# One x tile loaded behind wq instead of two ahead of it, the K folds in one row, the first keys right behind them

## The chip, the cores and the metric

The kernel runs on one core of a Trainium2 chip. The metric is the device time of one launch in microseconds (us), lower is better; a quoted time is the median of several runs. The profile's span, from the first to the last recorded instruction, is about 1.25 us shorter than the time of the same run (297.35 against 296.1).

Every profiled run has a granted clock of 1.0.

## The reference, cut to what matters

```python
qkv = x @ wqkv                                  # x: 2048 x 640, wqkv: 640 x 1920
pq, pk = einsum(q, w_phi), einsum(k, w_phi)     # per head, 32 heads of 20
phi_q = concat(softmax(pq), softmax(-pq)); phi_k likewise
kv = einsum(phi_k, v);  z = sum(phi_k)          # linear attention state
a = ((phi_q @ kv) / (phi_q @ z + 1e-6)) @ wo
b = (gelu(x @ w_gate) * (x @ w_up)) @ w_down
g = sigmoid((x * gate_w).sum(-1))
return g * a + (1 - g) * b
```

Since `q` and `k` are used only through `w_phi`, the kernel multiplies ("folds") `w_phi` into the q and k parts of `wqkv`. For this it needs both parts transposed, `wkT` and `wqT`. All of x is needed transposed as well (`xT`, 16 tiles of 128 rows). Tiles 0 to 3 are transposed by TensorE; tiles 4 to 15, `wkT` and `wqT` come through transposing DMAs, all issued by the SP queue.

## The kernel before: what the change touches

```python
def loads(self):                      # the order on the SP queue
    xload("sp", 0)                    # x tiles 0, 1, plain (2, 3: ACT queue)
    ...                               # five plain loads of the v weights
    xturn(4, 2)                       # transposing load of x tiles 4, 5
    wload(self.wkT, D, "wkT")         # transposing load, 640 x 640
    xturn(6, 2)                       # x tiles 6, 7
    wload(self.wqT, 0, "wqT")
    xturn(8, 4)
    xturn(12, 4)
    ...                               # weights of the feed-forward part

def fold(self, kt, which, banks, ekey):
    # six small matmuls of wT (k or q) with the block diagonal of w_phi, then one
    # copy out of PSUM into w3 (k) or wq2 (q), by VectorE ("d") or ScalarE ("a")
    ...

def attention_state(self):
    warm(7)                           # seven matmuls of zeros ahead of the work
    ...                               # transposes of x tiles 0..3, V of tiles 0..3
    self.v_early(4, 6)                # V projection of tile 4 into banks 6, 7
    self.v_early(5, 0)
    f(0, "k", (2, 3), "d")
    f(1, "k", (4, 5), "a")
    self.v_early(6, 6)
    f(2, "k", (2, 3), "d")
    f(3, "k", (4, 5), "a")
    f(4, "k", (0, 1), "d")
    self.v_early(7, 6)
    self.k_early(0, 2)                # K projection of tile 0, then two exponents on ScalarE
    f(0, "q", (4, 5), "d")
    f(1, "q", (6, 7), "d")
    ...                               # two folds, k_early(1), two folds, k_early(2), ...
    self.k_norm(0)                    # VectorE normalises phi_k of tile 0: 3.58 us
    self.k_early(3, 0)
    self.k_norm(1)
    self.pq(0, 1, 1)                  # Q product, banks 6/7 in turn, two exponents each
    self.pq(0, 0, 0)
    self.pq(0, 3, 3)
    self.gram(0)                      # phi_k^T v of tile 0, accumulated over all tiles
    self.k_norm(2)
    self.pq(0, 2, 2)
    ...
    for t in range(4, NT):            # projections of tile t, k_norm(t), Q products, and
        ...                           # Gram up to tile t-3 (t < 8), later up to tile t-2
```

A bank (0 to 7) is a part of PSUM, the memory that TensorE's products land in; copying a bank out is called evacuating it, and a product that needs the bank waits for that. A helper records every operation with the buffers that it reads and writes and places the waits. The names of the trace's lines are therefore those of helpers: L280 transposes of x, L350 V of tiles 0 to 3, L341 projection, L321 fold, L303 the gate column, L434 Gram, L486 Q product, L217 and L213 the transposing loads of x and of wk/wq. After the change everything behind the new method moves down by 9 lines (Gram is L443, the Q product L495), and L371 is that method.

The softmax here doesn't subtract the row's maximum and nothing guards it: scores larger than these inputs give would overflow.

## Time and profile before

| | before |
|---|---|
| time, 3 runs | 296.21 us (295.81 to 296.45) |
| the profiled run itself | 297.35 us, span 296.1 |
| PE busy | 291.0 us (98%) |
| V of tile 4 starts | 11.30 us |
| wait for x tiles 6 and 7 | 1.39 us |

The page's share of busy time shows that TensorE (PE) is the busiest by far (PEld is its weight load, DVE VectorE, ACT ScalarE, POOL GpSimd):

```profile
span 296.1 us, 4789 instructions
PE 291.0 (98%) x1904; PEld 169.1 (57%) x1904; DVE 162.7 (55%) x321; ACT 104.2 (35%) x183; POOL 27.8 (9%) x56
```

The timeline of PE in the block that the change touches (columns: start, duration, engine, line, operation, output and inputs, shape, count, and in brackets the idle time before it and what ended it):

```profile
4.47 1.29 PE L280 MATMUL ps<-ident,xtok 128*128 128x128 bf16 x20 [0.24 <-DMA xtok<-in_A_x_dram]
...
10.16 0.22 PE L303 MATMUL ps<-ident,gz 128*128 128x128 bf16 x1
...
11.30 2.88 PE L341 MATMUL ps<-w,xT 128*128 128x512 bf16 x20
14.02 0.79 PE L321 MATMUL ps<-BD,wkT 128*128 128x140 bf16 x12
16.20 1.53 PE L341 MATMUL ps<-w,xT 128*128 128x512 bf16 x10 [1.39 <-DMA xT<-in_A_x_dram]
17.57 1.11 PE L321 MATMUL ps<-BD,wkT 128*128 128x140 bf16 x18
...
29.64 1.25 PE L486 MATMUL ps<-xT,wq 128*128 128x512 bf16 x5 [0.34 <-ACT Eq L492]
```

V of tile 6 (16.20) waits 1.39 us for its transposed x. The SP queue's timeline shows why it came late: the load was issued at 10.66, behind 4.57 us of issue for wk (durations here are issue times, not data movement):

```profile
3.62 2.38 SPq L217 DMA_TRANSPOSE xT<-in_A_x_dram  x1
6.05 4.57 SPq L213 DMA_TRANSPOSE wkT<-in_A_wqkv_dram  x1
10.66 1.41 SPq L217 DMA_TRANSPOSE xT<-in_A_x_dram  x1
12.12 4.61 SPq L213 DMA_TRANSPOSE wqT<-in_A_wqkv_dram  x1
```

### The profile page before, as it was taken

To read this page: it belongs to the slowest core of one execution; us is meant where nothing else is said; L and a number is where in the kernel's file an instruction comes from. 1 tells how busy PE (TensorE), PEld (TensorE's weight loads), DVE (VectorE), ACT (ScalarE), POOL (GpSimd) and SP (SyncE) were. 2 spreads that over 40 slices of the span, in tenths; PEclk is the share of its full clock that TensorE was granted. 3 is DMA by queue.
4 is the path that set the end of the run, shared out by engine and by line. 5 is a ranking of instruction groups with operands and counts; after the bars stand their busy time and mean duration, and the time that the engine had idled before them with its cause. 6 is when DMAs were issued, how large, how long until landed. Compare 5 with 4: busy or idle time off the path is not lost.

```text
span 296.1 us, 4789 instructions
## 1 busy us (share of the span) xinstructions
PE 291.0 (98%) x1904; PEld 169.1 (57%) x1904; DVE 162.7 (55%) x321; ACT 104.2 (35%) x183; POOL 27.8 (9%) x56
## 2 busy tenths in 40 slices
PE   7989999999999999999999999999999999999997
PEld 3656565555554455766555567655556765555674
DVE  3238999998886579600777710077771007777100
ACT  3347787766773221112222211222221122222112
POOL 7000000000000011110111100012110001222000
PEclk9999999999999999999999999999999999999999
DMA  8999993000001302211011130101311000111111
GB/s 231 181 200 273 364 356 113 0 0 2 0 2 31 57 4 37 51 47 44 3 23 22 24 44 22 46 0 23 24 22 43 25 26 21 22 22 24 22 46 44
DMA packets 38224, 18.85 MB, mean 64 GB/s; under 512 B 30266, under 2 KB 37946, under 8 KB 38202
## 3 DMA queue, kind: packets, MB, share of 16 engines
q1 hardware_dynamic: 37392, 18.19, 25.0%
q10 hardware_dynamic: 810, 0.35, 0.4%
q8 instruction: 15, 0.25, 0.4%
q14 instruction: 7, 0.06, 0.1%
HBM read 9.04 MB, written 2.62 MB: 39 GB/s over the span
## 4 chain that ended last, share of the span: by engine, by line
PE 93%; SPq 3%; DMA 2%; ACT 1%; issue 0%; ACTq 0%
PE ps L594 38%; PE ps L693 19%; PE ps L341 12%; PE ps L699 8%; PE ps L486 7%; PE ps L630 4%; PE ps L434 3%; DMA xT<-in_A_x_dram 2%; SPq L213 2%; PE ps L604 1%; PE ps L672 1%; PE ps L321 1%; SPq L217 1%; SPq L226 1%; ACT Ek L400 0%; ACT Eq L492 0%
## 5 line engine op out<-in xcount | busy, mean ns | idle before, releaser
L599 DVE TENSOR_TENSOR hT<-ps,gl 128x512 bf16<-128x512 f32 x52 | 35.7, 688 | 79.8 <-PE ps L594 79.7
L594 PE MATMUL ps<-xT,wg_sb 128*128 128x512 bf16 x260 | 64.6, 379 | 0.0
L594 PE MATMUL ps<-xT,wu_sb 128*128 128x512 bf16 x260 | 64.6, 379 | 0.0
L597 ACT ACTIVATE gl<-ps 128x512 bf16<-128x512 f32 x52 | 31.1, 597 | 82.5 <-PE ps L594 80.3
L693 PE MATMUL ps<-wd_sb,hT 128*128 128x320 bf16 (+2 forms) x416 | 59.3, 299 | 0.0
L693 PEld LDWEIGHTS ps<-wd_sb,hT 128*128 128x128 bf16 x416 | 40.2, 98 | 16.8
L659 POOL TENSOR_TENSOR Og<-O,O 128x640 bf16<-128x640 bf16 x16 | 22.3, 1396 | 244.4 <-DVE O L657 244.4
L594 PEld LDWEIGHTS ps<-xT,wu_sb 128*128 128x128 bf16 x260 | 25.4, 98 | 30.7
L341 PE MATMUL ps<-w,xT 128*128 128x512 bf16 (+3 forms) x240 | 41.0, 321 | 1.4 <-DMA xT<-in_A_x_dram 1.4
L594 PEld LDWEIGHTS ps<-xT,wg_sb 128*128 128x128 bf16 x260 | 24.9, 98 | 26.4
L709 ACT ACTIVATE outsb<-ps,Gm 128x640 bf16<-128x640 f32 (+2 forms) x17 | 13.0, 763 | 71.5 <-PE ps L699 71.5
L341 PEld LDWEIGHTS ps<-w,xT 128*128 128x128 bf16 x240 | 22.3, 97 | 19.7 <-DMA xT<-in_A_x_dram 1.6
L411 DVE TENSOR_REDUCE Dk<-Ek 128x64 f32<-128x1280 bf16 x16 | 23.7, 1480 | 3.2 <-ACT gcol L403 3.2
L420 DVE TENSOR_TENSOR Ek<-Ek,Dk 128x640 bf16<-128x640 bf16 x32 | 25.0, 821 | 0.6
L486 PE MATMUL ps<-xT,wq 128*128 128x512 bf16 x100 | 24.7, 379 | 0.3 <-ACT Eq L492 0.3
L657 DVE TENSOR_TENSOR O<-ps,RH 128x640 bf16<-128x640 f32 x32 | 24.8, 815 | 0.0
L699 PE MATMUL ps<-wo_sb,goT 128*128 128x320 bf16 (+2 forms) x160 | 24.6, 299 | 0.0
L492 ACT ACTIVATE Eq<-ps 128x512 bf16<-128x512 f32 x40 | 21.7, 604 | 4.0 <-PE ps L486 4.0
L400 ACT ACTIVATE Ek<-ps 128x640 bf16<-128x640 f32 x32 | 20.7, 702 | 3.5 <-PE ps L341 3.5
L699 PEld LDWEIGHTS ps<-wo_sb,goT 128*128 128x128 bf16 x160 | 15.1, 98 | 7.2 <-issue 1.3
L630 PEld LDWEIGHTS ps<-KV,Eq 128*128 128x128 bf16 x192 | 12.0, 98 | 3.6
L630 PE MATMUL ps<-KV,Eq 128*128 128x154 bf16 x192 | 13.7, 221 | 0.0
(63 smaller groups left out, 148.4 us busy)
## 6 DMA issues: line engine op xcount, KB each, us to landing
out_dram<-outsb SPq DMA_DIRECT2D x15, 160.0 KB, 1.8
wd_sb<-in_B_w_down_dram SPq DMA_DIRECT2D x1, 2080.0 KB, 13.7
wg_sb<-in_B_w_gate_dram SPq DMA_DIRECT2D x1, 1120.0 KB, 6.1
wu_sb<-in_B_w_up_dram SPq DMA_DIRECT2D x1, 1120.0 KB, 8.5
wg_sb<-in_B_w_gate_dram SPq DMA_DIRECT2D x1, 960.0 KB, 9.8
wu_sb<-in_B_w_up_dram SPq DMA_DIRECT2D x1, 960.0 KB, 10.2
w<-in_A_wqkv_dram SPq DMA_DIRECT2D x5, 160.0 KB, 4.2
wo_sb<-in_A_wo_dram SPq DMA_DIRECT2D x1, 800.0 KB, 9.2
```

The source lines that it names most:

```text
L341: sc.op("pe", lambda e, kt=kt: e.matmul(self.bank(bank)[:, bcol:bcol + n], self.xT[:, kt, t * P:(t + 1) * P], self.w3[:, kt, c0:c0 + n], s ...
L411: sc.op("dve", lambda e: e.tensor_reduce(self.Dk[:, se, 0, :].rearrange("p (s h) -> p s h", h=H), self.Ek[:, se, :, :].rearrange("p s (h d ...
L420: sc.op("dve", lambda e, v=v, r=r: e.tensor_tensor(v, v, r, ALU.mult), reads=[("Rk", se)], writes=[("Ek", se, s)])
L486: sc.op("pe", lambda e, kt=kt: e.matmul(self.bank(bank), self.wq2[:, kt, i * P:(i + 1) * P], self.xT[:, kt, b * self.BT:(b + 1) * self.BT] ...
L594: sc.op("pe", lambda e, kt=kt, w=w, bk=bk: e.matmul(self.bank(bk), w[:, kt, c * P:(c + 1) * P], xs(kt), start=(kt == 0), stop=(kt == self. ...
L597: sc.op("act", lambda e: e.activation(self.gl[:, slot, :], self.bank(banks[0]), AF.Gelu_apprx_tanh), reads=[("ps", banks[0])], writes=[("g ...
L599: sc.op("dve", lambda e: e.tensor_tensor(self.hT[:, c, :], self.bank(banks[1]), self.gl[:, slot, :], ALU.mult), reads=[("ps", banks[1]), ( ...
L630: sc.op("pe", lambda e, s=s, i=i, n=n, o0=o0, k0=k0, bk=bk, r=r: e.matmul(self.bank(bk)[:, o0:o0 + n], self.Eq[:, s, i, t * P:(t + 1) * P] ...
L657: dve(lambda e, o=o, f=f, s=s: e.tensor_tensor(o, V[s][:, :, :, 0:DH], f, ALU.mult), rb + [key(6 + s)], [("O", s, sl)], guard=old)
L659: sc.op("pool", lambda e: e.tensor_tensor(self.Og[:, sl, :], self.O1[:, sl, :], self.O2[:, sl, :], ALU.add), reads=[("O", 0, sl), ("O", 1, ...
L693: sc.op("pe", lambda e: e.matmul(self.bank(bk, w), self.hT[:, c, tt * P:(tt + 1) * P], self.wd_sb[:, c, w0:w0 + w], start=(c == 0 and not ...
L699: sc.op("pe", lambda e: e.matmul(self.bank(bk, w), self.goT[:, gs, k, :], self.wo_sb[:, k, w0:w0 + w], start=False, stop=(k == self.KD - 1 ...
```

## The change

The intent is to take that wait away. Tile 6 is loaded with tiles 4 and 5 ahead of wk, so that three V projections can run before wk is needed; tile 7 moves behind wq and its V projection to the end of the block. All five K folds then run in a row. The first K projection follows them directly with the contraction tile as its outer loop, so that it can use each fold's copy as it comes. The Q folds are spread between the other K projections.

```diff
-        xturn(4, 2)
+        xturn(4, 3)
         wload(self.wkT, D, "wkT")
-        xturn(6, 2)
         wload(self.wqT, 0, "wqT")
+        xturn(7, 1)
         xturn(8, 4)
@@ new method
+    def k_behind(self, t, b0):
+        for kt in range(self.KD):
+            for c0, n, bk, col in ((640, 384, b0, 128), (1024, 257, b0 + 1, 0)):
+                ...                  # one matmul; waits only for ("wk2", kt)
+        self.k_evac(t, b0)
@@ attention_state
         self.v_early(4, 6)
         self.v_early(5, 0)
-        f(0, "k", (2, 3), "d")
-        f(1, "k", (4, 5), "a")
-        self.v_early(6, 6)
-        ...                          # three K folds
-        self.v_early(7, 6)
-        self.k_early(0, 2)
+        self.v_early(6, 2)
+        f(0, "k", (4, 5), "d")
+        f(1, "k", (6, 7), "a")
+        f(2, "k", (0, 1), "d")
+        f(3, "k", (2, 3), "a")
+        f(4, "k", (4, 5), "d")
+        self.k_behind(0, 6)
+        self.k_early(1, 0)
         f(0, "q", (4, 5), "d")
-        ...
+        ...                          # two q folds, k_early(2), two q folds, k_early(3), one q fold
         self.k_norm(0)
-        self.k_early(3, 0)
+        self.v_early(7, 0)
         self.k_norm(1)
         self.pq(0, 1, 1)
         self.pq(0, 0, 0)
         self.pq(0, 3, 3)
+        self.pq(0, 2, 2)
         self.gram(0)
         self.k_norm(2)
-        self.pq(0, 2, 2)
```

More of the change, by code (lines that the diff above doesn't have):

```diff
@@ L366, in v_first_evac @@
             self.sc.op("act", lambda e: e.activation(dst, src, AF.Copy), reads=rd, writes=wr)
+    def k_behind(self, t, b0):
+        for kt in range(self.KD):
+            for c0, n, bk, col in ((640, 384, b0, 128), (1024, 257, b0 + 1, 0)):
+                self.sc.op("pe", lambda e: e.matmul(
+                    self.bank(bk)[:, col:col + n], self.xT[:, kt, t * P:(t + 1) * P], self.w3[:, kt, c0:c0 + n],
+                    start=(kt == 0), stop=(kt == self.KD - 1)),
+                    reads=[("xT", t), ("wk2", kt), "wgate"], writes=[("ps", bk)], signal=(kt == self.KD - 1))
+        self.k_evac(t, b0)
     def k_early(self, t, b0):
@@ L540, in attention_state @@
         self.v_early(5, 0)
-        f(0, "k", (2, 3), "d")
-        f(1, "k", (4, 5), "a")
-        self.v_early(6, 6)
-        f(2, "k", (2, 3), "d")
-        f(3, "k", (4, 5), "a")
-        f(4, "k", (0, 1), "d")
-        self.v_early(7, 6)
-        self.k_early(0, 2)
-        f(0, "q", (4, 5), "d")
-        f(1, "q", (6, 7), "d")
-        self.k_early(1, 0)
-        f(2, "q", (4, 5), "d")
-        f(3, "q", (6, 7), "d")
-        self.k_early(2, 2)
-        f(4, "q", (4, 5), "d")
+        self.v_early(6, 2)
[6 more added lines that the diff above has]
+        self.k_early(1, 0)
+        f(0, "q", (4, 5), "d")
+        f(1, "q", (2, 3), "d")
+        self.k_early(2, 6)
+        f(2, "q", (0, 1), "d")
+        f(3, "q", (4, 5), "d")
+        self.k_early(3, 2)
+        f(4, "q", (6, 7), "d")
         self.k_norm(0)
-        self.k_early(3, 0)
+        self.v_early(7, 0)
         self.k_norm(1)
```

## The prediction

> **What bounds it now.** TensorE: the busy table gives PE 291.0 of 296.1 us, and in the chain of waits from 16.2 us to the end nearly every piece is PE. The granted clock is 1.0 throughout. So only PE idle time is to be had; in the part that the change touches (11.3 to 32.5 us) PE's timeline shows two gaps. (a) PE is idle 1.39 us before the V projection that starts at 16.20, released by the transposed load of x tiles 6 and 7: issued at 10.66, behind wk's 4.57 us of issue, it landed 5.49 us later. wk had landed at 13.35. (b) 0.34 us before the third Q product at 29.64, released by ScalarE's exponent.
>
> **What changes.** No arithmetic, bytes or number of loads. Tile 6 comes ahead of wk, tile 7 behind wq; folds and projections are reordered.
>
> *Loads.* On SP's timeline two tiles took 1.4 to 2.4 us to issue, four 3.3 to 3.5, wk and wq 4.6 each: about 0.75 us a tile. The Trainium skill (Perfetto Trace Analysis, "DMA Instruction — HWDGE") says that the reported duration ends when the descriptors are generated, not when data has moved; this trace agrees: wk's issue lasts 4.57 us, its landing takes 7.3. Landing came 2.7 to 3 us after the end of issue. My estimates: tiles 4 to 6 landed near 10.5; wk near 14.1 to 14.8 (before 13.35); wq near 18.8 (before 19.7); tile 7 near 21; tiles 8 to 15 about 1 us later, with over 15 us of slack.
>
> *TensorE.* A projection costs 1.36 us, a fold 0.315 (0.94 for three), a Q product 1.08, Gram 0.55. From 11.30: three V projections to 15.4, wk there in time by some 0.6 to 1.3 us; five K folds to about 17.0, the fifth waiting 0.1 to 0.2 for VectorE to evacuate banks 4 and 5 (0.82 a copy); the first K projection, contraction-tile-outer so that it can follow the folds' copies, waits for the last copy at about 18.3 and ends near 18.6, 0.3 late. The other K projections and the Q folds find banks, wq (needed at 20.0) and copies ready, ending near 24.3; V of tile 7 near 25.6, instead of 26.98. The Q products' exponent wait stays, 0.3 to 0.4; moving Gram 0 behind the fourth Q product adds at most 0.1. Block end near 31.0 instead of 32.5.
>
> VectorE's normalisations run back to back, 3.58 us a tile; they start about 1.3 us earlier and Gram 1 still finds its tile with 0.8 us to spare. From there on PE is unbroken, so the saving should arrive in full: 1.39 + about 0.4 of small gaps, less about 0.4 of new evacuation waits.
>
> **Predicted time: 294.8 us**, 8 in 10 between 294.1 and 296.0. Chance of faster by over 2%: 0.01; within 2%: 0.98; slower by over 2%: 0.01.
>
> **What would show it.** The wait for the transposed x tile on PE gone; V of tile 6 following tile 5 without gap; folds from 15.4; a wait of 0.1 to 0.5 us at the last K fold or inside the first K projection, released by VectorE or ScalarE; no wait on wk or wq; first Gram near 30.5; everything later shifted by the same 1.4 us; DMA and busy totals unchanged.
>
> **What would make it wrong.** wk or wq landing over 1 us later than estimated, so that the wait just moves to the folds: then 0 to 0.8 us of gain. Evacuation waits in the folds above 1 us. VectorE's normalisations, nearly saturated until 50 us, holding Gram.

## The result

| | before | after |
|---|---|---|
| time, 6 runs each | 296.33 us (295.81 to 297.44) | 296.86 us (295.92 to 297.01) |
| the profiled run, and its span | 297.35, 296.1 us | 296.78, 295.5 us |
| gate column (L303) starts | 10.16 us | 10.98 us |
| gate column to the end | 285.94 us | 284.52 us |

The ratio is 1.0005, 95% interval 0.9981 to 1.0029: the same. (A ratio here is the mean time of one kernel's fast runs over that of the other's of the same rounds, so it is not quite the ratio of the medians.) The predicted 294.8 with 294.1 to 296.0 missed; the time did not go down at all.

Yet the profile after shows nearly everything that was foretold. PE's timeline of the changed kernel:

```profile
4.56 2.06 PE L280 MATMUL ps<-ident,xtok 128*128 128x128 bf16 x20
...
10.98 0.22 PE L303 MATMUL ps<-ident,gz 128*128 128x128 bf16 x1
...
12.33 4.02 PE L341 MATMUL ps<-w,xT 128*128 128x512 bf16 x29
16.19 1.95 PE L321 MATMUL ps<-BD,wkT 128*128 128x140 bf16 x30
17.98 1.60 PE L371 MATMUL ps<-w,xT 128*128 128x384 bf16 x10
...
26.44 4.75 PE L495 MATMUL ps<-xT,wq 128*128 128x512 bf16 x20
31.03 0.71 PE L443 MATMUL ps<-Ek,vaug 128*128 128x240 bf16 x6
```

The three V projections run without a gap (x29 and not x30: one record is missing, and the true start is about 12.12), the folds follow, no DMA is waited for. The SP queue, same columns as before:

```profile
3.62 3.29 SPq L217 DMA_TRANSPOSE xT<-in_A_x_dram  x1
6.95 3.84 SPq L213 DMA_TRANSPOSE wkT<-in_A_wqkv_dram  x1
10.83 3.87 SPq L213 DMA_TRANSPOSE wqT<-in_A_wqkv_dram  x1
14.74 8.90 SPq L217 DMA_TRANSPOSE xT<-in_A_x_dram  x3
```

And the page's first lines:

```profile
span 295.5 us, 4764 instructions
PE 290.8 (98%) x1879; PEld 169.7 (57%) x1904; DVE 162.6 (55%) x321; ACT 104.5 (35%) x183; POOL 27.7 (9%) x56
```

To compare runs, cut each at a point that both kernels share and that lies ahead of the change: the start of the gate column. What comes before it is the "head", identical in both kernels; what comes after it is the "tail". Between these two profiles the tail fell by 1.42 us (285.94 to 284.52), which is the predicted 1.4. The head grew by 0.82, although the change does not touch it. So two questions are left: why does the head move, and why do the timed runs show nothing of the tail's 1.42?

### The profile page after: what moved, and what is told of

Read it like the earlier page. It is cut to its first block, busy times and chain, and to the rows that moved or that the text cites. A ratio compares the mean times of both kernels' runs of the same rounds, so it can differ in the third digit from the quotient of the medians.

```text
span 295.5 us, 4764 instructions
## 1 busy us (share of the span) xinstructions
PE 290.8 (98%) x1879; PEld 169.7 (57%) x1904; DVE 162.6 (55%) x321; ACT 104.5 (35%) x183; POOL 27.7 (9%) x56
## 2 busy tenths in 40 slices
DMA packets 38224, 18.85 MB, mean 64 GB/s; under 512 B 30266, under 2 KB 37946, under 8 KB 38202
## 4 chain that ended last, share of the span: by engine, by line
PE 97%; DMA 1%; issue 1%; ACT 0%
PE ps L603 38%; PE ps L702 19%; PE ps L341 12%; PE ps L708 8%; PE ps L495 7%; PE ps L639 4%; PE ps L443 3%; PE ps L350 2%; PE ps L613 1%; DMA xtok<-in_A_x_dram 1%; PE ps L321 1%; PE ps L681 1%; PE ps L280 1%; PE ps L371 0%; ACT Eq L501 0%
## 5 line engine op out<-in xcount | busy, mean ns | idle before, releaser
L603 PE MATMUL ps<-xT,wg_sb 128*128 128x512 bf16 x251 | 63.0, 380 | 0.5
L341 PE MATMUL ps<-w,xT 128*128 128x512 bf16 (+3 forms) x228 | 39.0, 322 | 0.1
L341 PEld LDWEIGHTS ps<-w,xT 128*128 128x128 bf16 x230 | 21.5, 97 | 17.6
L495 PE MATMUL ps<-xT,wq 128*128 128x512 bf16 x94 | 23.4, 380 | 0.4
```

The source lines that it names most:

```text
L341: sc.op("pe", lambda e, kt=kt: e.matmul(self.bank(bank)[:, bcol:bcol + n], self.xT[:, kt, t * P:(t + 1) * P], self.w3[:, kt, c0:c0 + n], s ...
L495: sc.op("pe", lambda e, kt=kt: e.matmul(self.bank(bank), self.wq2[:, kt, i * P:(i + 1) * P], self.xT[:, kt, b * self.BT:(b + 1) * self.BT] ...
L603: sc.op("pe", lambda e, kt=kt, w=w, bk=bk: e.matmul(self.bank(bk), w[:, kt, c * P:(c + 1) * P], xs(kt), start=(kt == 0), stop=(kt == self. ...
```

## The experiments

Theory A: the 1.39 us wait was an accident of the one profiled run of before; the timed runs mostly don't have it, so there is nothing to save. Theory B: the wait is typical and the gain real, but hidden by a random stretch of slow TensorE clock in the head. Theory C: the gain is real at 32 us and given back later, because VectorE's back-to-back normalisations hold the Gram products. Twelve runs were made, all correct.

All tails and heads, from PE's timeline and the span of each profile:

| run | head | tail | PE's waits for DMA behind the head |
|---|---|---|---|
| before, first profile | 10.16 | 285.94 | x tiles 6, 7: 1.39 |
| null_before | 10.34 | 284.36 | none |
| look_b2 | 10.79 | 284.41 | none |
| look_b3 | 10.66 | 284.34 | none |
| late_before | 18.61 | 284.39 | none |
| after, first profile | 10.98 | 284.52 | none |
| after_again | 10.90 | 284.60 | none |
| after_third | 10.10 | 284.60 | none |
| late_after | 18.85 | 284.55 | none |
| order_only | 10.55 | 284.55 | none |
| tuned | 11.16 | 284.34 | none |
| loads_only | 10.90 | 286.0 | x tile 7: 1.50 |
| delay_before | 10.20 | 286.8 | wk 1.02, x tiles 6, 7: 0.99 |
| delay_after | 10.21 | 285.39 | wk: 0.66 |

### 1. The kernel before again (null_before)

Edit: none; timed in 5 rounds.

> The kernel before, unchanged, timed against itself: it shows the scatter that any verdict has to be read against, and gives a second profile. Theory A (the profiled run of before had an unusually late wait for x tiles 6 and 7, 1.39 us): in this second profile that wait is shorter, under 0.8 us. Theory B (the wait is typical and the saving of about 1.4 us is real, but lost in the timed runs to an early stretch of slow TensorE clock that falls at random): the wait is again 1.2 to 1.5 us, and the timed runs fall in two groups 0.7 to 1.0 us apart. Ratio to before 1.000 within 0.003 either way.

Measured: ratio 0.9998 (0.9983 to 1.0013), 295.64 to 296.86. PE's timeline of this profile:

```profile
11.48 2.88 PE L341 MATMUL ps<-w,xT 128*128 128x512 bf16 x20
14.20 0.79 PE L321 MATMUL ps<-BD,wkT 128*128 128x140 bf16 x12
14.83 1.52 PE L341 MATMUL ps<-w,xT 128*128 128x512 bf16 x10
16.19 1.11 PE L321 MATMUL ps<-BD,wkT 128*128 128x140 bf16 x18
...
28.25 1.25 PE L486 MATMUL ps<-xT,wq 128*128 128x512 bf16 x5 [0.34 <-ACT Eq L492]
```

V of tile 6 follows the folds with no wait at all. The SP queue of the same run says why: wk took 3.80 us to issue instead of 4.57, and the load behind it was issued 0.9 us earlier and landed after 4.7 us instead of 5.49, at 14.46: 0.37 us before it was needed.

```profile
3.62 2.25 SPq L217 DMA_TRANSPOSE xT<-in_A_x_dram  x1
5.91 3.80 SPq L213 DMA_TRANSPOSE wkT<-in_A_wqkv_dram  x1
9.76 1.41 SPq L217 DMA_TRANSPOSE xT<-in_A_x_dram  x1
11.21 5.52 SPq L213 DMA_TRANSPOSE wqT<-in_A_wqkv_dram  x1
```

What follows: theory A. The same instructions have a tail of 284.36 us, 1.58 shorter than in the first profile, and 0.16 shorter than the changed kernel's.

### 2. The changed kernel again (after_again)

Edit: none; 5 rounds.

> The changed kernel, unchanged, a second time. Theory B: its runs again fall in groups 0.7 to 1.0 us apart, according to whether the 20 transposes of x by TensorE took 1.3 us (fast clock) or about 2.1 us (slow clock); over ten runs of each kernel the mean gain shows, ratio 0.996 to 0.998. Theory A: no groups needed, ratio 0.999 to 1.001, and this profile shows the same block length as the first one.

Measured: ratio 1.0004 (0.9991 to 1.0018), five runs: 296.71, 296.86, 296.63 and 296.06, 296.13. Theory B's mean gain did not come; its two groups did, and its slow transposes: the 20 took 2.22 us in this profile, which belongs to the run of 296.71.

### 3 and 4. Both kernels behind a long warm-up (late_before, late_after)

```diff
+        sc.op("dve", lambda e: e.memset(self.zero[:, :], 0.0), writes=["zero"])
+        for i in range(26):
+            sc.op("pe", ...matmul of zeros..., reads=["zero"], writes=[("ps", 0), "pre"])
         xload("sp", 0)               # now with reads=["pre"]
...
-        warm(7)
+        warm(14)
```

> The kernel before with 26 extra warming matmuls ahead of the first load, which waits for them, and 14 instead of 7 behind it: the real work starts with TensorE's clock already up, so the random stretch of slow clock is gone. Costs about 7 us, the same in both late kernels. Transposes 1.3 us in every run, timed runs within 0.5 us of each other if the clock was the scatter (theory B). Its profile shows the wait for x tiles 6 and 7: 1.2 to 1.5 us by theory B, under 0.8 by theory A.

> The changed kernel with the same late, warm start. Theory B: 1.2 to 1.6 us faster than late_before (ratio of the two 0.995 to 0.996). Theory A: within 0.5 us of late_before. Theory C (the gain is real at 32 us but VectorE's back-to-back normalisations hold the Gram products and give it back by 60 us): the block to the first Gram is 1.6 us shorter, the end less than 1.0 us earlier.

Measured: 304.34 us (303.34 to 304.75, 4 runs) and 304.30 us (303.54 to 305.02, 5 runs); ratios to before 1.0265 and 1.0264. Both profiles have transposes of 1.29 us and no wait for DMA; tails 284.39 and 284.55. Theory B's gain of 1.2 to 1.6 us is not there, so theory A holds here too. My expectation of runs within 0.5 us of each other was a miss: they scatter by 1.4 to 1.5 us. The loads now wait for the warm-up, whose length varies too (26 matmuls took 8.12 us in one profile, 8.30 in the other), so part of the scatter may only have moved ahead of everything. The two profiles show 0.18 us of it there, so where the rest comes from is not shown.

### 5 and 6. Late loads on purpose (delay_before, delay_after)

```diff
         xturn(4, 2)                  # delay_after: xturn(4, 3)
+        xturn(8, 2)                  # loaded again later; only takes the queue's time
         wload(self.wkT, D, "wkT")
```

> The kernel before with one more transposed load of two x tiles (8 and 9, loaded again later) behind the first, so that wk, x tiles 6 and 7 and wq all land an estimated 1.4 to 2.5 us later (1.41 us of issue, 2.9 us from wk's landing to that of the two tiles). Insurance theory (the change moves the deadlines of the loads and gains only what the loads would have cost): the undelayed profile had 0.37 us to spare for x tiles 6 and 7 and 0.23 us for wq, so PE now waits 1.0 to 2.3 us in this block in every run; 1.0 to 2.0 us slower than before. Rival (the waits of before are rare and PE work hides such a delay): within 0.5 us of before.

> The changed kernel with the same extra load at the same place. Its profiles left 2.4 to 3.0 us to spare for wk and 2.6 to 3.1 for wq. Insurance theory: PE waits 0 to 0.3 us, time within 0.5 us of the changed kernel without the delay and 1.0 to 2.0 us below delay_before (ratio of the two 0.993 to 0.997). Rival: the two delayed kernels within 0.5 us of each other.

Measured: delay_before 298.19 us (297.95 to 300.39), ratio 1.0082 (1.0054 to 1.0110); delay_after 297.38 us (296.88 to 297.84), ratio 1.0039 (1.0022 to 1.0056). The ratio of the two through the same runs of before is 1.0039 / 1.0082 = 0.9957, inside the expected 0.993 to 0.997. But delay_before's two slowest runs are those with the clock of 0.994. Without them its mean is 1.7 us above before, that of delay_after 1.0, and the ratio of the two is 0.9976, just outside. By that count delay_after is 0.7 us below delay_before, where I expected 1.0 to 2.0, and some 0.9 above the changed kernel without the delay (in other rounds), where I expected at most 0.5: both missed. The order of the two is clear all the same: the slowest run of delay_after (297.84) is below the fastest of delay_before (297.95). PE of delay_before, then of delay_after:

```profile
15.24 0.80 PE L322 MATMUL ps<-BD,wkT 128*128 128x140 bf16 x12 [1.02 <-DMA wkT<-in_A_wqkv_dram]
17.04 1.53 PE L342 MATMUL ps<-w,xT 128*128 128x512 bf16 x10 [0.99 <-DMA xT<-in_A_x_dram]
```

```profile
11.35 4.24 PE L342 MATMUL ps<-w,xT 128*128 128x512 bf16 x30
16.25 1.96 PE L322 MATMUL ps<-BD,wkT 128*128 128x140 bf16 x30 [0.66 <-DMA wkT<-in_A_wqkv_dram]
```

What follows: the change is an insurance. When the loads are late, it saves part of the loss: 0.7 of 1.7 us in the timed runs (those of clock 0.994 left out), 1.6 of 2.4 in the two profiles, by tails that are 2.4 and 0.8 us longer than those of the undelayed kernels. The expected 0 to 0.3 us of waiting for delay_after was too low: wk landed at 16.2 us (8.24 + 8.0), 2.4 to 3.1 us later than in the three profiles of the changed kernel (13.8, 13.1, 13.6), where I had estimated 1.4 to 2.5.

### 7 and 8. One half of the change each (loads_only, order_only)

loads_only takes the new order of the loads with TensorE's old order; order_only takes TensorE's new order with the loads of before.

> Only the order of the loads changed (three tiles, wk, wq, fourth tile), TensorE's order as before. Tile 7 then lands 9 to 9.8 us after wk's issue ends, at about 19.2 us, and is needed at 17.2 us: a wait of about 2 us on PE for the transposed x tile, 1.5 to 2.2 us slower than before. If the load order alone were the gain it would be the same or faster.

> Only TensorE's order changed (three V projections, five K folds, and so on), loads as before. Tile 6 is needed at 14.2 us and lands between 14.5 and 16.1: a wait of 0.3 to 1.9 us for the transposed x tile, wk and wq always in time. 0.3 to 1.5 us slower than the changed kernel.

Measured, loads_only: 298.41 us (298.12 to 300.70), ratio 1.0086 (1.0055 to 1.0118); without the run of 300.70 (clock 0.994) the mean is 1.9 us above before, inside the expected 1.5 to 2.2. Tile 7, now behind wq, is too late for TensorE's old order, by 1.50 us where I expected about 2:

```profile
19.36 2.89 PE L341 MATMUL ps<-w,xT 128*128 128x512 bf16 x20 [1.50 <-DMA xT<-in_A_x_dram]
```

Measured, order_only: 296.47 us, ratio 1.0015 (0.9989 to 1.0042); the runs were 296.37, 296.13, 296.57 and 298.17. My expectation of a wait in every run was a miss: in the profile the load of tiles 6 and 7 was issued at 9.51 and landed 4.8 us later, at 14.3, and V of tile 6 needed it at 14.4. The tail is 284.55, that of the changed kernel. The run of 298.17 may be one in which that 0.1 us did not suffice; it has no profile, so this is not shown.

### 9. Two small repairs (tuned)

```diff
-        f(4, "q", (6, 7), "d")
+        f(4, "q", (0, 1), "d")
         self.k_norm(0)
-        self.v_early(7, 0)
         ...
         self.pq(0, 0, 0)
+        self.v_early(7, 4)
         self.pq(0, 3, 3)
...
-                    for g in range(g, t - 2 if t < 8 else t - 1):
+                    for g in range(g, t - 2 if t < 10 else t - 1):
```

> The changed kernel with two small repairs: V of tile 7 moved between the second and third Q product, where PE waited about 0.4 us for ScalarE's exponent, and the Gram products kept two tiles behind up to tile 9, so that Gram 6 no longer waits 0.2 us for VectorE's normalisation. From the first V projection of tile 4 to the end it took 283.4 us in the changed kernel and 283.2 in the undisturbed profile of before; if the two waits are what they seem, 282.9 to 283.1 here. Timed 0.3 to 0.6 us below the changed kernel in the same rounds, 0 to 0.4 below before: at the edge of what the rounds can tell.

Measured: 296.70 us (296.40 to 296.85), ratio 1.0003 (0.9989 to 1.0017); after_third in the same rounds 1.0000 (0.9987 to 1.0014). By the clock it is neither better nor worse than the others. Its tail is 284.34, 0.2 shorter than the changed kernel's and equal to that of an undisturbed before. From V of tile 4 that makes 283.2 us, so the expected 282.9 to 283.1 was missed as well: with V of tile 7 gone from there, the first Q product now waits for wq's last copy (the wait view puts 0.6 us there on the weight load, PEld). It is no version that beats both.

### 10. The changed kernel a third time (after_third)

> The changed kernel a third time, beside the tuned one. If its scatter is the clock's, then runs near 296.0 and near 296.8, and this profile's time goes with how long the 20 transposes took (1.3 us: 296.0; 2.1 us: 296.8). From the first V projection of tile 4 to the end 283.3 to 283.5 us, whatever the head.

Measured: 295.91, 296.50, 296.71, 296.81, 296.80; the profiled run was the one of 295.91, and its transposes took 1.29 us, as expected. The tail is 284.60; the expected range was met (from V of tile 4 at about 11.24, 283.5). Here is the lines view's grouping of the head's matmuls in the first profile after and in this one (line, shape, count, busy us, mean ns):

```profile
L350 PE MATMUL ps<-w,xT 128*128 128x160 bf16 x20 | 4.7, 233 | 0.0
L280 PE MATMUL ps<-ident,xtok 128*128 128x128 bf16 x20 | 2.1, 292 | 0.1
```

```profile
L350 PE MATMUL ps<-w,xT 128*128 128x160 bf16 x20 | 4.7, 233 | 0.0
L280 PE MATMUL ps<-ident,xtok 128*128 128x128 bf16 x20 | 1.3, 220 | 0.1
```

The transposes differ by 0.8 us and the seven matmuls of zeros ahead of them by 0.2 (3.2 against 3.0 us in the same view); the V matmuls behind them take the same 233 ns. The head varies from 10.10 to 11.16 us over the twelve profiles with the normal start, and the three profiled times of the changed kernel go with it: heads 10.10, 10.90, 10.98, times 295.91, 296.71, 296.78.

### 11 and 12. Two more looks at the kernel before (look_b2, look_b3)

> The kernel before, one more look: is the wait of 1.39 us for x tiles 6 and 7 rare? Expected no wait or one below 0.5 us, the load of tiles 6 and 7 landing within 0.6 us of the moment that PE needs it.

> As the look before it: a wait below 0.5 us. If this or the other look shows over 1 us, the wait is common and the timed runs should show it too.

Measured: 296.42 and 296.31 us; no wait for any load in either. Tiles 6 and 7 landed at 13.4 and 14.3 us and were needed at 15.28 and 15.14, so the expected closeness of 0.6 us was a miss: they were 1.9 and 0.8 us early. Five profiles of the kernel before (one of them with the late start) now show the wait once.

## Why the prediction was wrong, point by point

- **TensorE bounds the kernel, and only PE's idle time is to be had:** right. PE is 98 to 99% busy in every profile of both kernels.
- **What the change does in that block:** right. No gap at tile 6, no wait for wk or wq, folds in a row. The loads came earlier than I estimated: wk at 13.1 to 13.8 against 14.1 to 14.8, wq at 17.6 to 18.4 against 18.8. The Trainium skill (Perfetto Trace Analysis, "DMA Instruction — HWDGE") says that a DMA's reported duration covers its issue and not its data; every profile agrees (wk: 3.84 us of issue, 6.8 to landing).
- **Sizes of the small waits:** nearly right in the block. From V of tile 4 to the first Q product the undisturbed before took 14.11 us (11.48 to 25.59), the changed kernel 14.33 in its second profile (12.04 to 26.37): 0.22 lost, where I had 0.4 for evacuation waits (the wait view puts 0.2 us on the first K projection's weight load, waiting for a fold's copy by VectorE). From there to the K projection of tile 4, 5.37 against 5.13: 0.24 won, where I had 0.4.
- **"From there on PE is unbroken, so the saving should arrive in full":** not quite. Theory C is true on a small scale. PE got the 0.22 us of evacuation waits back from the smaller exponent wait, but VectorE's chain of normalisations did not: it begins 13.98 us behind V of tile 4 (26.02 against 12.04, second profile), in null_before 13.76 (25.24 against 11.48). It then runs without a break up to Gram 6, which waits for it. PE's pair of Gram products in null_before and in the changed kernel, second profile:

```profile
49.95 1.26 PE L434 MATMUL ps<-Ek,vaug 128*128 128x240 bf16 x12
```

```profile
50.49 1.47 PE L443 MATMUL ps<-Ek,vaug 128*128 128x240 bf16 x12
```

and the wait view of the first profile after names it:

```profile
PEld ps L443 <- DVE Ek L429: 0.2, 1, 0.2
```

  I had checked Gram 1 only. The wait stands in all five profiles with TensorE's new order and without tuned's repairs, and in none of before. Those 0.2 us are the difference of the tails: 284.52 to 284.60 in the changed kernel, 284.34 to 284.41 in the undisturbed before. Lagging the Gram products (tuned) took the pause away, and the tail came back to 284.34; that run moved V of tile 7 as well, so the two are not apart.
- **The step that failed** is the first term of the sum: "the saving should arrive in full: 1.39". The wait was put down as a property of the kernel; it was one of that run. It is real there (the tail fell by 1.42 between the first two profiles), but four other profiles of the same kernel have none of it (0 us), and its timed runs were already as fast as the changed kernel's. The warning was in the data: the profiled run took 297.35 us, the timed ones 295.81 to 296.45. A wait of 1.39 us in a run that is about 1.1 us slow is the first suspect for the slowness, not a cost of all runs.
- **What would make it wrong** named three things; none of them was that the wait need not be there.

Over all runs quoted here of the unchanged kernels with the normal start (first profiled run of before left out), 45 of before have a mean of 296.42 and 16 of after 296.54. The tail of an undisturbed run plus the head (10.1 to 11.2) plus 1.25 gives 295.7 to 296.8 for before; 3 of the 45 runs are above 297.1 and would fit the wait, but they have no profile, so its frequency is an inference. The record does not name the chip of the first rounds; the four profiles without the wait come from chips 13 and 4. That the wait belongs to a chip is unlikely, though not excluded: five of the six timed runs of before in those first rounds took 295.81 to 296.78 us.

A tail is not wholly independent of its head. The first transposing load is issued at 3.62 us in all twelve profiles with the normal start, whatever the head, so a longer head leaves a late load more time. The first profile of before had the shortest head of the four (10.16); with the 10.79 of look_b2 the same late load would have cost an estimated 0.8 us and not 1.39 (1.39 less 0.63). That the tail fell by just the predicted amount is in part luck.

Why the wait came in the first profile is not fully settled. What that profile shows is a late first transposed load (landed 6.2 us after issue, 4.6 to 5.4 in the other profiles of before with the normal start) with a hole in the DMA traffic behind it. Here are the stretches from 8.5 to 10 us of the first profile, then from 14.5 to 16 us of null_before (the last two columns are DMA share and GB/s; only the GB/s are used here):

```profile
8.50:9.00 0.50, 0.50 (x6) 0.29 (x5) 0.00 (x0) 0.00 (x0) 0.00 (x0) 1.00 2.91 89
9.00:9.50 0.50, 0.50 (x5) 0.33 (x4) 0.00 (x0) 0.00 (x0) 0.00 (x0) 1.00 0.09 5
9.50:10.00 0.50, 0.50 (x6) 0.34 (x4) 0.00 (x0) 0.00 (x0) 0.00 (x0) 1.00 0.79 161
```

```profile
14.50:15.00 0.50, 0.50 (x11) 0.43 (x8) 0.22 (x1) 0.50 (x1) 0.00 (x0) 1.00 3.81 54
15.00:15.50 0.50, 0.50 (x4) 0.22 (x3) 0.50 (x1) 0.50 (x2) 0.00 (x0) 1.00 0.04 4
15.50:16.00 0.50, 0.50 (x5) 0.26 (x4) 0.11 (x1) 0.29 (x1) 0.00 (x0) 1.00 0.08 9
```

In the first profile almost nothing moved for half a microsecond (5 GB/s), where null_before moved 248 to 290 GB/s between 8.5 and 10 us. Behind it wk landed at 13.35 (12.3 in null_before) and tiles 6 and 7 at 16.15 (14.46). Such a hole is nothing special: null_before has a longer one, and after_third has one in the same place (2 and 9 GB/s from 15 to 16 us). But these two came when wk and the tiles loaded ahead of wq had landed. Only wq was left to be late, and in null_before it still came 0.2 us before its first fold. So what sets the first profile apart is that its hole came early. No run here provokes a hole or moves one, so that this made the wait is inferred and not shown.

The head's scatter has an explanation that fits: the Trainium skill (TensorE: Matmul & The Clock Gate, "What's actually happening") says that the clock comes up after a busy window which is free-running, so the moment varies from run to run, by its figures ±500 ns. The profiles agree in kind: the same 20 transposes took 1.29 to 2.32 us, and the head's spread is 1.06 us. Both first profiles of the changed kernel had the slow ones and the first of before the fast ones; look_b2 and look_b3 (2.06 and 1.94 us) and after_third (1.29) show that this goes with no kernel. Behind the long warm-up both late profiles have 1.29 us, which fits as well; but their timed runs scatter no less, so that this alone makes the scatter of the times is not shown.

## What to carry to other kernels

Before a wait in a profile is counted as a gain, compare the profiled run's own time with the timed runs, and look at a second profile: a wait on a DMA whose landing lies close to its need is there in one run and gone in the next. Compare tails from a common point ahead of the change rather than whole spans; here that told 0.2 us apart where the timed runs scatter by more than 1. If a load is waited for behind that point, compare only tails with like heads. A change that only moves deadlines of loads is an insurance: measure it with the loads made late, and don't expect it to pay when they are not.

## What the Trainium skill lacked or had wrong

- DMA: Bandwidth & Descriptors, "Latency and other measured facts", states bandwidths and fixed costs but no scatter of one and the same transposing load. Here the first load of two x tiles took 1.53 to 2.38 us to issue and landed after 4.6 to 6.2 us (four profiles of before with the normal start); wk took 3.72 to 4.57 us to issue. Nor has it the holes: 2 to 9 GB/s over stretches of 0.5 to 1 us in three profiles, at 9.0 us or at 15.0.
- The same section gives 261 GB/s for a transposing DMA with a non-contiguous middle dimension, and about 350 to 400 for the contiguous case; no run here tells which case these loads are. The 0.5 us stretches in which only such loads were moving ran at up to 292 GB/s, with stretches of 68 to 105 GB/s towards the end of each load (first profile of before, 10 to 23 us). The page's figures may still hold for a whole load; the two phases are not there.
- TensorE: Matmul & The Clock Gate, "What you observe", has the random wake-up with ±500 ns. Nothing wrong with it. The page distrusts a trace's clock events in general, but has no case like this one: the granted clock stood at 1.00 in every stretch of the head in the first profiles of before and after, while the same 20 transposes took 1.29 us in the one and 2.06 in the other.
- Perfetto Trace Analysis, "Optimization Strategy", tells to find the gaps of the contended engine and what ends them. It lacks the step that failed here: to check that a gap is in more than one run (1.39 us in one profile of before, none in four others).
